# Decode attention with a gated MLP: wq's first block on ScalarE's queue

## The chip, the core and the metric

The kernel runs on one core of a Trainium2 chip. A core has TensorE (matrix multiplications, PE in the profile), VectorE (DVE), ScalarE (ACT), GpSimd (POOL) and SyncE (SP), and 16 DMA engines that move data between the chip's memory and the core's own memory of 128 partitions. SyncE and ScalarE each have a queue on which they issue transfers; in the profile SyncE's is q1 and ScalarE's is q10. The metric is device time in microseconds (us), less is better.

## What is computed

One decode step for 8 sequences: attention over the last 1024 of 4096 cached positions, with 16 query heads on 8 key heads of width 256, and beside it an MLP on the normalised input, mixed by a gate.

```python
# x [8, 1, 448], k_cache and v_cache [8, 8, 4096, 256], wq [448, 4096], wo [4096, 448]
g = _sigmoid((x * gate_w).sum(-1, keepdims=True))
q = (x @ wq).reshape(B, Sq, Hq, Dh).transpose(0, 2, 1, 3)
k = jnp.repeat(k_cache[:, :, Sk - W:, :], rep, axis=1)      # W = 1024, rep = 2
v = jnp.repeat(v_cache[:, :, Sk - W:, :], rep, axis=1)
scores = jnp.einsum("bhqd,bhkd->bhqk", q, k) * (Dh ** -0.5)
o = jnp.einsum("bhqk,bhkd->bhqd", _softmax(scores), v)
a = o.transpose(0, 2, 1, 3).reshape(B, Sq, Hq * Dh) @ wo
y = _layernorm(x)
b = _gelu(y @ w1 + b1) @ w2 + b2
return g * a + (1 - g) * b
```

All tensors are bfloat16.

## The kernel before

Everything large goes through one ring of four slots of 32 KB on each of 128 partitions (4 MB a slot). A list `plan`, filled by `add` (lines 108 to 110), holds the loads in their order: wq; the keys of batch 0; then for each batch b from 1 to 7 its keys and the values of batch b-1; the first MLP weight; the last values and the second MLP weight; wo. `pump` (line 98) issues the loads for which a slot is free, and `done` (line 104), called when the work on a slot has been written, issues the next one; on the chip that load waits until the slot's last reader has finished. So at the start four loads are issued at once: wq, the keys of batches 0 and 1, the values of batch 0. The keys of batch 2 go into wq's slot after the query product, the values of batch 1 into that of batch 0's keys, and so on.

wq has 448 rows. Rows 0 to 383 lie three to a partition (`wq_m`, line 147), so that a partition's three rows are 24 KB in a piece of memory. They are loaded in two pieces (`wq_r`, line 155): the first row of each partition, 8 KB, 1 MB in all; the second and third, 16 KB, 2 MB in all. The last 64 rows, each in two halves, are a third piece (`wq_t`, 4 KB a partition). `rows_loader` (line 137) issues these pieces one behind the other on SyncE's queue; it is also used for the first MLP weight and for wo.

The small inputs are x (8 rows of 896 bytes, line 181) and the gate's row, copied to 8 partitions (line 185), both on ScalarE's queue, and the biases, later, on SyncE's.

`moments` (line 253) brings x into the form that TensorE needs: VectorE copies it into `xs` (lines 228 and 232), transposes it (line 234) and copies the result into `xw` (line 239). It then takes mean and variance, and ScalarE a square root (line 257), for which it loads a table. `query` (line 383) multiplies: 24 matmuls (line 389), the first eight with wq's first piece, the other sixteen with the second, and four (line 401) with the third. ScalarE scales the product (line 411), VectorE transposes it (line 414), both copy it into `qw` (line 427), and `gate` computes the gate from x and the gate's row.

Then, for each batch, TensorE transposes the keys (line 370), ScalarE and VectorE copy the results out of the accumulation memory (lines 376 and 378), GpSimd copies the blocks that VectorE transposed (lines 338 and 346), and TensorE forms the scores (line 435) and, one batch later, the weighted values (line 506). The order of the work on each engine is as written (`manual_schedule`). At the end come the MLP, the product with wo in pieces (lines 662 and 679), the sum (line 689) and the output, half on SyncE's and half on ScalarE's queue (line 691).

Of the kernel before, what the change touches and what calls it, by code (L numbers as in the profile page):

```python
# [17 lines left out]
def kernel(  # L18
# [15 lines left out]
    nc = tc.nc  # L34
# [73 lines left out]
    def add(key, loader):  # L108
        index[key] = len(plan)
        plan.append(loader)  # L110
# [4 lines left out]
    def half_loader(src, b):  # L115
        def load(t):
            for i in range(NG):
                v = src[b, i:Hkv:NG, kv_base:Sk, :].rearrange(
                    "a (s c) d -> s a (c d)", c=NCK
                )  # L120
                nc.sync.dma_start(t[:, i * HS : (i + 1) * HS], v)

        return load
# [10 lines left out]

        return load

    def rows_loader(pieces):
        def load(t):
            o = 0
            for ap in pieces:  # L140
                n = ap.shape[-1]
                nc.sync.dma_start(t[:, o : o + n], ap)  # L142
                o += n

        return load

    wq_m = A_wq[0:DM, :].rearrange("(p r) n -> p (r n)", r=NR)
    wq_t = A_wq[DM:D, :].rearrange("r (h n) -> (r h) n", h=2)
# [6 lines left out]
    wq_r = [wq_m[:, 0:HD], wq_m[:, HD : NR * HD]]  # L155

    def last_values(t):
        pair_loader(A_v_cache, NB - 1, 2)(t)
        nc.sync.dma_start(slot("w12")[:, OW2 : OW2 + FB * D], w2_v)

    add(("wq",), rows_loader(wq_r + [wq_t]))
    add(("k", 0), half_loader(A_k_cache, 0))
    for b in range(1, NB):
        add(("k", b), (half_loader if b == NB - 1 else pair_loader)(A_k_cache, b))
        add(("v", b - 1), pair_loader(A_v_cache, b - 1))
    add(("w12",), rows_loader([w1_m, w1_t]))
    add(("v", NB - 1), last_values)
    cuts = [(q, 0, J8) for q in range(NQW - 2)] + [
# [5 lines left out]
        (NQW - 1, 7, 8),  # L174
    ]
    add(("wo",), rows_loader([wo_v[:, q, j0 * D : j1 * D] for q, j0, j1 in cuts]))

    x_sb = consts.tile([NB, D], BF16)
# [543 lines left out]
```

## Time and profile before

| | |
|---|---|
| time, median of 3 runs | 189.98 us (189.89 to 190.21) |
| profiled execution: its own time | 189.76 us |
| profiled execution: span from the first to the last instruction | 188.0 us |
| busy time TensorE / VectorE / ScalarE / GpSimd | 122.3 / 96.5 / 91.4 / 66.4 us |
| moved by the DMA engines | 77.85 MB, mean 414 GB/s |
| packets on q1 (SyncE) / q10 (ScalarE) | 6712 / 48 |
| TensorE's granted clock, mean share | 0.873 |

The span is what the profile sees on the core; the execution's own time holds what lies around it as well. A busy share is an average over the whole span, so the stages have to be looked at one by one. In a timeline, a row of a "DMA" instruction on ACTq or SPq is the time in which that engine issued the transfer, not the time in which the data moved; an idle time in brackets is followed by what ended it. In the chain of waits, a step "DMA" runs from the issue to the landing and so holds the time in the queue.

### The profile page before, as it was taken

To read this page: it belongs to the slowest core of one execution; us is meant where nothing else is said; L and a number is where in the kernel's file an instruction comes from. 1 tells how busy PE (TensorE), PEld (TensorE's weight loads), DVE (VectorE), ACT (ScalarE), POOL (GpSimd) and SP (SyncE) were. 2 spreads that over 40 slices of the span, in tenths; PEclk is the share of its full clock that TensorE was granted. 3 is DMA by queue.
4 is the path that set the end of the run, shared out by engine and by line. 5 is a ranking of instruction groups with operands and counts; after the bars stand their busy time and mean duration, and the time that the engine had idled before them with its cause. 6 is when DMAs were issued, how large, how long until landed. Compare 5 with 4: busy or idle time off the path is not lost.

```text
span 188.0 us, 2799 instructions
## 1 busy us (share of the span) xinstructions
PE 122.3 (65%) x1104; PEld 79.8 (42%) x1104; DVE 96.5 (51%) x166; ACT 91.4 (49%) x115; POOL 66.4 (35%) x143
## 2 busy tenths in 40 slices
PE   0273099598598447991695948923968885353972
PEld 0022096395296216750684336503853662110221
DVE  7306514754287926740673248713763773763511
ACT  2006879598249255862287059620891994010000
POOL 8000093291069505800398039100991840000000
PEclk9999759969969997999579699995799999955599
DMA  6999999999999999999999999999999999999991
GB/s 211 448 411 439 446 422 422 436 443 422 422 439 424 420 436 439 422 422 439 436 425 425 443 432 418 429 443 436 411 436 446 415 425 428 416 429 441 412 402 54
DMA packets 6771, 77.85 MB, mean 414 GB/s; under 512 B 588, under 2 KB 1128, under 8 KB 1896
## 3 DMA queue, kind: packets, MB, share of 16 engines
q1 hardware_dynamic: 6712, 77.68, 97.3%
q8 instruction: 8, 0.13, 0.2%
q10 hardware_dynamic: 48, 0.02, 0.0%
q14 instruction: 3, 0.02, 0.0%
HBM read 77.69 MB, written 0.01 MB: 413 GB/s over the span
## 4 chain that ended last, share of the span: by engine, by line
DMA 76%; PE 13%; POOL 5%; DVE 2%; ACT 1%; issue 1%; SPq 0%; POOLq 0%; DVEq 0%
DMA slot<-in_A_k_cache_dram 51%; DMA slot<-in_A_v_cache_dram 12%; DMA slot<-in_A_wo_dram 9%; PE ktp L370 8%; POOL kt L346 5%; DMA slot<-in_A_wq_dram 5%; DVE kt L378 1%; PE S_ps L435 1%; ACT kt L376 1%; PE S_ps L389 1%; PE S_ps L401 1%; PE PO L506 1%; DVE B L338 1%; PE S_ps L679 0%; SPq L142 0%
## 5 line engine op out<-in xcount | busy, mean ns | idle before, releaser
L370 PE MATMUL ktp<-ident_f,slot 128*128 128x128 f32 x468 | 73.3, 314 | 33.3 <-DMA slot<-in_A_k_cache_dram 21.2
L346 POOL COPY kt<-B 32x128 f32<-32x128 f32 (+1 forms) x128 | 62.1, 485 | 85.9 <-DVE B L338 80.9
L376 ACT COPY kt<-ktp 128x1024 bf16<-128x1024 bf16 x77 | 73.3, 1030 | 27.4 <-PE ktp L370 27.0
L370 PEld LDWEIGHTS ktp<-ident_f,slot 128*128 128x128 f32 x468 | 61.4, 162 | 47.9 <-issue 21.6
L378 DVE COPY kt<-ktp 128x1024 bf16<-128x1024 bf16 x40 | 27.5, 687 | 19.0 <-PE ktp L370 18.9
L435 PE MATMUL S_ps<-kt,qw 128*4 128x512 bf16 x256 | 17.4, 412 | 7.6 <-POOL kt L346 6.2
L506 PE MATMUL PO<-slot,ET 128*16 128x512 bf16 x256 | 17.5, 416 | 7.3 <-DMA slot<-in_A_v_cache_dram 7.3
L453 ACT ACTIVATE E<-S_ps,nmx 128x1024 f32<-128x1024 f32 x8 | 8.9, 1114 | 22.9 <-DVE nmx L448 22.9
L448 DVE TENSOR_REDUCE nmx<-S_ps 128x1 f32<-128x1024 f32 x8 | 9.8, 1224 | 17.9 <-PE S_ps L435 17.9
L338 DVE STREAM_TRANSPOSE B<-slot 128x512 f32<-128x512 f32 (+1 forms) x8 | 7.3, 908 | 21.2 <-DMA slot<-in_A_k_cache_dram 21.2
L506 PEld LDWEIGHTS <-ET 128*16 128x16 bf16 x256 | 7.1, 94 | 16.8 <-issue 11.0
L435 PEld LDWEIGHTS <-qw 128*4 128x4 bf16 x256 | 5.9, 85 | 16.0 <-issue 10.6
L462 DVE STREAM_TRANSPOSE EB<-E 128x1056 f32<-128x1056 f32 x8 | 10.2, 1278 | 0.3
L389 PE MATMUL S_ps<-slot,xw 128*8 128x512 bf16 x24 | 2.9, 617 | 9.4 <-DVE xw L239 6.0
L522 DVE STREAM_TRANSPOSE T<-PO 128x512 f32<-128x512 f32 x8 | 5.6, 703 | 3.6 <-PE PO L506 3.6
L489 DVE TENSOR_TENSOR ET<-sm,mask 128x512 bf16<-128x512 f32 x8 | 5.5, 692 | 3.4 <-PE sm L481 3.4
L414 DVE STREAM_TRANSPOSE qt<-qs 128x512 bf16<-128x512 bf16 x2 | 1.3, 690 | 8.7 <-ACT qs L411 8.7
L389 PEld LDWEIGHTS <-xw 128*8 128x8 bf16 x24 | 0.6, 100 | 10.7 <-POOL b_r L222 5.9
L584 ACT ACTIVATE zb<-za 128x448 f32<-128x448 f32 x1 | 0.6, 577 | 8.5 <-DVE za L583 8.5
L651 PE MATMUL warm<-slot,ident 128*128 128x512 bf16 (+1 forms) x12 | 4.6, 475 | 0.0
L411 ACT ACTIVATE qs<-S_ps 128x1024 bf16<-128x1024 f32 x1 | 1.0, 1023 | 7.3 <-PE S_ps L401 7.3
L468 DVE SCALAR_TENSOR_TENSOR EZ<-EB,gall 128x128 bf16<-128x128 f32 x8 | 4.0, 495 | 0.0
(81 smaller groups left out, 57.6 us busy)
## 6 DMA issues: line engine op xcount, KB each, us to landing
slot<-in_A_v_cache_dram SPq DMA_DIRECT2D x7, 4096.0 KB, 31.1
slot<-in_A_k_cache_dram SPq DMA_DIRECT2D x6, 4096.0 KB, 37.7
slot<-in_A_k_cache_dram SPq DMA_DIRECT2D x4, 2048.0 KB
slot<-in_A_v_cache_dram SPq DMA_DIRECT2D x2, 2048.0 KB
slot<-in_A_wq_dram SPq DMA_DIRECT2D x1, 2048.0 KB
slot<-in_A_wo_dram SPq DMA_DIRECT2D x2, 896.0 KB
slot<-in_B_w_dram SPq DMA_DIRECT2D x1, 1568.0 KB
slot<-in_B_w_dram SPq DMA_DIRECT2D x1, 1344.0 KB, 22.2
```

The costliest lines, as they stand in the source:

```text
L338: nc.vector.transpose(B[:].rearrange("p c w s a -> p (c w s a)"), kn[:, 0 : n * P],)
L346: nc.gpsimd.tensor_copy(words[BL * w : BL * (w + 1), :, 0:n, g * S8 : (g + 1) * S8, 0], B[BL * g : BL * (g + 1), :, w].rearrange("p c s a ...
L370: nc.tensor.transpose(words[:, c, :, 0], kn[:, o : o + P], ident_f[:])
L376: nc.scalar.copy(dst, src)
L378: nc.vector.tensor_copy(dst, src)
L435: nc.tensor.matmul(S_ps[BL * t : BL * t + UR, n * QN : (n + 1) * QN], lhsT=qw[:, j, b, t, rep * u : rep * u + UR], rhs=KT[u][:, t, n * CQ ...
L448: nc.vector.reduce_max(nmx[:], S_ps[:], axis=AXIS.X, negate=True)
L453: nc.scalar.activation(E[:, 0:W], S_ps[:], ACT.Exp, bias=soft.pop(b)[:], scale=1.0, accum_out=total[:],)
L462: nc.vector.transpose(EB[:].rearrange("p c r -> p (c r)"), E[:])
L489: nc.vector.tensor_tensor(ET[:].rearrange("p c u a r -> p (c u) a r"), sm[:] .rearrange("p k (o r) -> p k o r", o=1) .to_broadcast([P, NCK ...
L506: nc.tensor.matmul(PO[BL * t : BL * t + Hq], lhsT=ET[:, c].rearrange("p u a r -> p (u a r)"), rhs=vn[:, c], start=(c < QD), stop=(c >= NCK ...
L522: nc.vector.transpose(T[:, 0 : NG * n], PO[:].rearrange("p u (e j) -> p u j e", j=J8))
```

## The change

`rows_loader` takes an engine for its first piece, and wq's call names ScalarE. So wq's first piece (128 rows of 8 KB) is issued on ScalarE's queue; since `pump` runs before line 181, it stands ahead of x and the gate's row there. wq's second piece is the first transfer on SyncE's queue. The loads of the first MLP weight and of wo stay wholly on SyncE's queue.

```diff
-    def rows_loader(pieces):
+    def rows_loader(pieces, first=nc.sync):
         def load(t):
             o = 0
-            for ap in pieces:
+            for i, ap in enumerate(pieces):
                 n = ap.shape[-1]
-                nc.sync.dma_start(t[:, o : o + n], ap)
+                eng = nc.sync if i else first
+                eng.dma_start(t[:, o : o + n], ap)
                 o += n
 
         return load
...
-    add(("wq",), rows_loader(wq_r + [wq_t]))
+    add(("wq",), rows_loader(wq_r + [wq_t], nc.scalar))
```

The new lines of `rows_loader` shift the later lines of the file by one.

## The prediction

> **What bounds the kernel now.** I read the page first, then the chain of waits in order of time, then the first 15 us instruction by instruction, because the change touches only transfers issued in the first 2 us.
>
> ```profile
> span 188.0 us, 2799 instructions
> GB/s 211 448 411 439 446 422 422 436 443 422 422 439 424 420 436 439 422 422 439 436 425 425 443 432 418 429 443 436 411 436 446 415 425 428 416 429 441 412 402 54
> q1 hardware_dynamic: 6712, 77.68, 97.3%
> DMA 76%; PE 13%; POOL 5%; DVE 2%; ACT 1%; issue 1%; SPq 0%; POOLq 0%; DVEq 0%
> ```
>
> Each of the 40 slices is 4.7 us. From the second to the last but one the transfers run at 402 to 448 GB/s without a hole, and one queue, q1 (SyncE's), carries 77.68 MB of it at 97.3% of the 16 DMA engines. TensorE, the busiest compute engine, is busy 65% of the span. So the span is: the time until the stream runs, plus 77.7 MB at about 430 GB/s, plus what follows the last byte. The chain shows that tail:
>
> ```profile
> 14.21 37.71 DMA slot<-in_A_k_cache_dram
> ...
> 167.62 16.71 DMA slot<-in_A_wo_dram
> 184.33 0.04 issue
> 184.37 0.88 PE S_ps L679 x12
> ```
>
> The columns are start, duration, what. The last piece of wo lands at 184.33, twelve matmuls end it, and 3.7 us after the landing the span is over. The step at 14.21 is not a 37 us transfer: the keys of batch 2 are issued the moment the query product frees the slot of wq, and queue behind three slots of 4 MB. That queueing is the cover for everything below.
>
> The start, as the timeline has it (start, duration, engine, line, what; in brackets the idle time before it and what ended it):
>
> ```profile
> 0.73 0.59 ACTq L181 DMA_DIRECT2D x_sb<-in_A_x_dram  x1
> 0.73 1.35 SPq L142 DMA_DIRECT2D slot<-in_A_wq_dram  x3
> 2.41 0.54 DVE L228 COPY xs<-x_sb 8x384 bf16<-8x384 bf16 x1
> 5.96 1.02 PE L389 MATMUL S_ps<-slot,xw 128*8 128x512 bf16 x8 [5.96 <-DVE xw L239]
> 10.44 1.88 PE L389 MATMUL S_ps<-slot,xw 128*8 128x512 bf16 x16 [3.46 <-DMA slot<-in_A_wq_dram]
> 12.25 1.92 PE L401 MATMUL S_ps<-slot,xw 128*72 128x512 bf16 x4
> ```
>
> x goes through VectorE from 2.41 to the first matmul at 5.96, 3.55 us. Eight matmuls use wq's first block; the other twenty wait until 10.44 for the second block, so x has slack today. The windows say how the stream comes up (bounds, length, five engines' busy time, clock, DMA share, GB/s):
>
> ```profile
> 1.70:3.00 1.30, 0.00 (x0) 0.00 (x0) 1.25 (x6) 1.25 (x1) 1.30 (x5) 1.00 0.94 212
> 3.00:10.00 7.00, 1.02 (x8) 0.26 (x9) 3.42 (x9) 0.29 (x1) 1.96 (x5) 1.00 0.99 421
> 20.00:50.00 30.00, 23.33 (x205) 17.55 (x205) 13.78 (x24) 22.87 (x29) 12.71 (x32) 0.83 1.00 430
> ```
>
> Nothing moves before 1.70. Against 430 GB/s the ramp loses 1.30 x (1 - 212/430) = 0.66 us, and the 7 us after it 0.15 us: 0.8 us in all is what a perfect start could win.
>
> **The change, part by part.** No byte, no instruction on TensorE, VectorE or GpSimd and no later transfer is added or taken away. Three things move.
>
> *SyncE's queue loses one issue.* Its three wq issues took 1.35 us, so 0.45 each; the second and third and the first four key and value issues come 0.45 us earlier. Worth nothing: behind the first issue there is always a backlog (the last of these transfers ends after 37 us).
>
> *ScalarE's queue gains a 128-row issue at its head.* Estimate 0.4 to 0.6 us, from SyncE's 0.45 and from ScalarE's own first issue of 0.59. x's issue moves from 0.73 to about 1.3, the gate row's from 1.36 to about 1.6, and the table load at 1.67 to about 2. The table is wanted only by the square root at 6.69: hidden. The first byte doesn't move: today both queues issue at 0.73 and their first packets follow in the window 1.70 to 3.00; then too both issue at 0.73. Zero for the stream, with the ramp's own uncertainty from -0.8 (all of its loss is filled) to +0.66 (the second queue pays such a ramp again, on the same engines). I take 0, since nothing in the rows says that the ramp is short of queued work: wq's first block alone gives each engine eight rows of 8 KB, 2.4 us of work.
>
> The Trainium skill (DMA: Bandwidth & Descriptors, section "Issuing engines are not separate DMA queues") says that transfers of all issuing engines end up on the same 16 DMA engines, and that issuing from several saves only sequencer time. By that rule the change saves 0.45 us of issue that nobody waits for, which speaks against a gain; the ramp's 0.8 us is what the rows would still allow.
>
> *x now stands behind 1 MB on its queue, and that megabyte shares the engines with q1.* This is the real cost. What a second queue gets beside q1 is shown by the gate row, issued from 1.36 to 1.64. The packets of ScalarE's queue, q10, from three windows, 1.6 to 1.9, 5.4 to 5.8 and 6.05 to 6.4:
>
> ```profile
> q10 hardware_dynamic: 16, 0.01, 9.0%
> q10 hardware_dynamic: 8, 0.01, 5.1%
> q10 hardware_dynamic: 8, 0.00, 1.3%
> ```
>
> The sixteen early ones are x (eight rows and eight completion writes). The gate's eight rows were served only from 5.4, after wq's first block, and its completions one large packet later. So q10 is not passed over for good, but can wait behind about nine packets of q1, and then gets about every other turn.
>
> An engine moves 430/16 = 26.9 GB/s: 0.305 us for an 8 KB row of wq's first block, 0.61 us for a 16 KB row of its second. Eight rows of each per engine. When x lands:
> - first block served first: 1.7 + 0.66 + 8 x 0.305 = 4.8 us;
> - turn and turn about: 1.7 + 0.66 + 8 x 0.92 = 9.7, and 1.2 for x's row and its completion behind one 16 KB packet each: 10.9 us;
> - q1's eight rows first, as with the gate: 2.4 + 8 x 0.61 + 8 x (0.305 + 0.15 for the 4 KB rows of wq's tail) + 1.2 = 12.1 us.
>
> From x it is 3.55 us to the first matmul and then 28 matmuls without a wait, 1.02 + 1.88 + 1.92 = 4.8 us: the query ends 8.4 us after x, against 14.2 today. First case: no slip. Second: 19.3, a slip of 5.1 us. Third: 20.5, a slip of 6.3. I take the second, and keep 0 and 6.3.
>
> The Trainium skill (the same page, "Queues, rings and completion order") has the engines go round robin between queues at packet granularity. By that, x lands at 10.9; by the gate's row, 12.1; the span is the same by both.
>
> *Where the slip goes.* All of ScalarE's and VectorE's work on q, the transposes of key slots 0 and 1 and so the issues of later slots move by up to 6.3 us. What is late next would be the stream, if a slot were issued after the queue has run dry. The tightest issue, and three rows of how TensorE stands to the stream later:
>
> ```profile
> 45.96 0.65 SPq L131 DMA_DIRECT2D slot<-in_A_k_cache_dram  x1
> 52.05 2.25 PE L370 MATMUL ktp<-ident_f,slot 128*128 128x128 f32 x10 [2.49 <-DMA slot<-in_A_k_cache_dram]
> 71.56 3.78 PE L370 MATMUL ktp<-ident_f,slot 128*128 128x128 f32 x20 [2.16 <-DMA slot<-in_A_k_cache_dram]
> 91.02 5.35 PE L370 MATMUL ktp<-ident_f,slot 128*128 128x128 f32 x24 [5.69 <-DMA slot<-in_A_k_cache_dram]
> ```
>
> When the keys of batch 3 are issued at 45.96, wq's 3.5 MiB and five slots of 4 MiB are queued before them, 24.6 MB; at 430 GB/s from 2.5 us they last until 59.8. Less about 1 us from issue to first packet, 12.8 us remain. A slip of 5.1 uses less than half. TensorE then waits 2.49 us less for batch 2, 2.16 less for batch 3 and the rest, 0.45, is gone at batch 4. From 91 us on nothing differs. Cost 0; without this cover it would be 5.1 us.
>
> Sum: span 188.0 + 0, with the 1.76 around it 189.76, the profiled execution's own time. The median shown, 189.98, is 0.22 above that: forecast 190.0.
>
> **The rivals.**
> - *The ramp fills.* Two queues put twice the reads in flight while the first packets come back, and 0.4 to 0.8 us of the loss goes: 189.2 to 189.6, middle 189.4. For it: 212 GB/s in that stretch. Against: x's sixteen packets were in that ramp too, and q1 had work queued on every engine. Chance 0.17.
> - *A second ramp* (slower). The second queue pays its start on the same engines, in the place of q1's packets: +0.4 to +0.66 us, 190.4 to 190.6. For it: the 1.70 to 3.00 row has no cause that the trace shows. Against: the gate's rows at 5.4 left the rate of 3 to 10 at 421. Chance 0.15.
> - *The stream runs dry* (slower). If q10 gets one packet in four, not in two, its eight rows take 8 x (0.305 + 3 x 0.61) = 17.1 us, x lands at 2.4 + 17.1 + 3.7 = 23.2 and the slip is 17.4. It decides from a slip of 12.8, that is from x landing at 18.6; past that every microsecond shows: 17.4 - 12.8 = +4.6, 194.6. For it: the gate waited behind nine packets. Against: its completion waited behind one. Chance 0.10.
>
> **How the numbers follow.** Forecast "hidden", 190.0, chance 0.58. A measurement of this kernel can tell about 0.2% (0.38 us) from no change; only the ramp rival is faster by more (0.17), the second ramp and the dry stream are slower (0.25). The range goes from 190.0 - 0.8 = 189.2 to 190.0 + 0.66 + 0.2 for the spread of the runs shown = 190.9, and leaves the dry stream outside.
>
> **What would show it.** Right: in the changed profile x's copy on VectorE starts near 11 us and not at 2.41, the query ends near 19, the keys of batch 2 are issued there, the GB/s row has no hole, and TensorE's wait for batch 2 is shorter or gone while the wait for batch 4 is as before. The ramp rivals are read from the GB/s of 1.70 to 10. Wrong: a slice under 400 GB/s near 60 us, or a different landing of wo's last piece.

## The result, and the profile after

The changed kernel takes 190.31 us (median of 15 runs), the kernel before in the same series 189.97 us (15 runs): a ratio of 1.0018, with a 95% interval of 1.0011 to 1.0025. That is 0.34 us slower: less than the 0.2% that the prediction took as the least that can be told from no change, but over these 15 runs the interval leaves out 1. The profiled execution took 190.5 us, its span 188.8.

From the page of the changed kernel, lines as in the prediction:

```profile
span 188.8 us, 2798 instructions
GB/s 198 432 421 441 424 437 424 441 427 424 434 430 429 422 431 430 434 434 424 427 441 424 434 427 434 431 420 437 434 431 427 424 437 421 416 427 437 418 385 29
q1 hardware_dynamic: 6568, 76.63, 95.7%
q10 hardware_dynamic: 192, 1.07, 1.4%
DMA 56%; PE 22%; DVE 8%; POOL 5%; ACT 4%; issue 2%; ACTq 0%; DVEq 0%; POOLq 0%
```

The stream still has no hole, and q10 now carries wq's first block. The first slice is lower (198 for 211). The share of DMA in the chain of waits fell from 76% to 56%, since the chain now goes through x, the query and TensorE's work up to 62 us, where it had the 37.71 us step of the keys of batch 2 before. Such a step holds the time in the queue, so the fall doesn't mean that less time is bound by the stream: the GB/s row is as full as it was.

Six rows of the changed kernel's start, from its timeline:

```profile
1.17 0.59 ACTq L182 DMA_DIRECT2D x_sb<-in_A_x_dram  x1
11.21 0.61 SPq L131 DMA_DIRECT2D slot<-in_A_v_cache_dram  x1
11.49 0.54 DVE L229 COPY xs<-x_sb 8x384 bf16<-8x384 bf16 x1 [8.97 <-DMA x_sb<-in_A_x_dram]
14.06 2.73 PE L390 MATMUL S_ps<-slot,xw 128*8 128x512 bf16 x24 [14.06 <-DVE xw L240]
16.73 1.92 PE L402 MATMUL S_ps<-slot,xw 128*72 128x512 bf16 x4
18.68 0.61 SPq L131 DMA_DIRECT2D slot<-in_A_k_cache_dram  x1
```

x, issued at 1.17, reaches VectorE at 11.49, not at 2.41. The 28 matmuls then run without a wait, the query ends at 18.65, and the keys of batch 2 are issued at 18.68, not at 14.21: a slip of 4.5 us. The same slip two batches on, and where it ends:

```profile
50.37 0.65 SPq L131 DMA_DIRECT2D slot<-in_A_k_cache_dram  x1
...
53.91 2.93 PE L371 MATMUL ktp<-ident_f,slot 128*128 128x128 f32 x20
...
71.84 1.50 PE L371 MATMUL ktp<-ident_f,slot 128*128 128x128 f32 x12 [0.75 <-DMA slot<-in_A_k_cache_dram]
91.80 3.43 PE L371 MATMUL ktp<-ident_f,slot 128*128 128x128 f32 x15 [6.97 <-DMA slot<-in_A_k_cache_dram]
```

The keys of batch 3 are issued at 50.37 (before 45.96), still 4.4 us late. TensorE's wait for batch 2 is gone (2.49 before), that for batch 3 is 0.75 (2.16), and at batch 4 TensorE waits again, longer than before (6.97 for 5.69): it is ahead of the stream, and the stream itself is late. So the slip is not seen in the loss; e2 below tests that. Two windows of the changed kernel, with the bounds used before:

```profile
3.00:10.00 7.00, 0.00 (x0) 0.00 (x0) 0.00 (x0) 0.41 (x1) 1.87 (x5) 1.00 0.97 408
20.00:50.00 30.00, 19.01 (x142) 16.26 (x141) 15.79 (x38) 23.93 (x35) 12.83 (x32) 0.77 1.00 430
```

From 3 to 10 us the engines moved 408 GB/s, not 421: 7 x 13/430 = 0.2 us lost. (The windows and the GB/s row count a row of a transfer where it starts.) From 20 us on the rate is the same 430. The end of the chain of waits:

```profile
168.27 16.77 DMA slot<-in_A_wo_dram
185.05 0.04 issue
185.09 0.89 PE S_ps L680 x12
```

wo's last piece lands at 185.05, before at 184.33; the tail behind it is unchanged. This execution is 0.19 us above its kernel's median, so its 0.72 is more than the typical loss.

What the packets' own records in the trace say is used in the experiments. The first row that each engine moved took 520 to 1085 ns in the kernel before (8 KB; 309 ns later on), and 856 to 1767 ns in the changed one (16 KB, from q1; 611 ns later on), with rows of q10 up to 1024 ns behind it. And the completions of the second half of batch 0's keys, one for each engine, spread from 20.69 to 21.03 us before and from 20.70 to 21.70 after. The first engine is no later; the last one is 0.67 us later, near the 0.72 by which wo's last piece is later. When the keys of batch 1 land near 31 us, the spread between the first and the last engine is still the same, 0.34 us before and 1.00 after: an engine that falls behind in the ramp stays behind.

### The profile page after: what moved, and what is told of

It reads as the page before. It is cut to its first block, busy times and chain, and to the rows that moved or that the text cites. A ratio compares the mean times of both kernels' runs of the same rounds, so it can differ in the third digit from the quotient of the medians.

```text
span 188.8 us, 2798 instructions
## 1 busy us (share of the span) xinstructions
PE 120.4 (64%) x1104; PEld 78.1 (41%) x1104; DVE 94.6 (50%) x166; ACT 90.8 (48%) x115; POOL 66.7 (35%) x143
## 4 chain that ended last, share of the span: by engine, by line
DMA 56%; PE 22%; DVE 8%; POOL 5%; ACT 4%; issue 2%; ACTq 0%; DVEq 0%; POOLq 0%
DMA slot<-in_A_k_cache_dram 30%; PE ktp L371 14%; DMA slot<-in_A_v_cache_dram 12%; DMA slot<-in_A_wo_dram 9%; DMA x_sb<-in_A_x_dram 5%; POOL kt L347 5%; DVE kt L379 4%; PE S_ps L436 3%; PE PO L507 2%; PE S_ps L390 1%; ACT qw L428 1%; ACT kt L377 1%; PE S_ps L402 1%; DVE B L339 1%; DVE qt L415 1%
## 5 line engine op out<-in xcount | busy, mean ns | idle before, releaser
L371 PE MATMUL ktp<-ident_f,slot 128*128 128x128 f32 x468 | 70.3, 305 | 32.0 <-DMA slot<-in_A_k_cache_dram 16.1
L371 PEld LDWEIGHTS ktp<-ident_f,slot 128*128 128x128 f32 x468 | 58.9, 157 | 45.7 <-issue 18.2
L507 PE MATMUL PO<-slot,ET 128*16 128x512 bf16 x256 | 18.3, 430 | 7.1 <-DMA slot<-in_A_v_cache_dram 7.1
L436 PE MATMUL S_ps<-kt,qw 128*4 128x512 bf16 x256 | 18.1, 429 | 6.9 <-POOL kt L347 6.9
L229 DVE COPY xs<-x_sb 8x384 bf16<-8x384 bf16 x1 | 0.5, 541 | 9.0 <-DMA x_sb<-in_A_x_dram 9.0
```

What stands on the lines that cost most here:

```text
L371: nc.tensor.transpose(words[:, c, :, 0], kn[:, o : o + P], ident_f[:])
L436: nc.tensor.matmul(S_ps[BL * t : BL * t + UR, n * QN : (n + 1) * QN], lhsT=qw[:, j, b, t, rep * u : rep * u + UR], rhs=KT[u][:, t, n * CQ ...
L507: nc.tensor.matmul(PO[BL * t : BL * t + Hq], lhsT=ET[:, c].rearrange("p u a r -> p (u a r)"), rhs=vn[:, c], start=(c < QD), stop=(c >= NCK ...
```

## The experiments

Each ratio is against the kernel before in the same series, with its 95% interval.

### One part at a time

**e1**, x and the gate's row ahead of wq's first block on ScalarE's queue:

```diff
     x_sb = consts.tile([NB, D], BF16)
-    pump()
     nc.scalar.dma_start(x_sb[:], xf)
...
     nc.scalar.dma_start(g_b[:], ...)
+    pump()
```

> x and the gate's row stand ahead of wq's first block on ScalarE's queue; wq is still on two queues. The changed kernel measured 1.0018 of the one before, and in its profile 7 us from 3.0 on ran at 408 GB/s, not 421. Theory A (the large piece at the head of SyncE's queue: the first packet of an engine is 16 KB, not 8 KB, and takes 0.9 to 1.8 us, not 0.5 to 1.1): SyncE's queue still begins with 16 KB rows, so 1.001 to 1.002. Theory B (two bulk queues in the ramp cost a second start): 1.001 to 1.002. Theory C (x late, and with it the slip of 4.5 us of the work up to batch 4): x lands near 2 us, so 1.000. By all three the first matmul is at about 6 us and the query ends between 14 and 16 us.

Measured: 1.0009 (1.0001 to 1.0018). Half of the loss, though x is early; the query ends at 16.1 us, not within the 14 to 16 expected.

**e2**, one bulk queue, x late:

```diff
-    add(("wq",), rows_loader(wq_r + [wq_t]))
+    def wq_then_x(t):
+        rows_loader(wq_r + [wq_t])(t)
+        nc.sync.dma_start(x_sb[:], xf)
+        nc.sync.dma_start(g_b[:], ...)
+    add(("wq",), wq_then_x)
...
-    nc.scalar.dma_start(x_sb[:], xf)
...
-    nc.scalar.dma_start(g_b[:], ...)
```

> All of wq on SyncE's queue in the old order, x and the gate's row behind it on the same queue; ScalarE's queue is empty until the output. x lands near 11 us and the query ends near 19 us, as in the changed kernel, but one queue does the ramp and its first packets are 8 KB. Theory A: 1.000. Theory B: 1.000. Theory C: 1.0018, the whole of the changed kernel's loss.

Measured: 1.0001 (0.9992 to 1.0010). In its timeline x and the query are as late as in the changed kernel:

```profile
11.97 0.54 DVE L231 COPY xs<-x_sb 8x384 bf16<-8x384 bf16 x1 [9.45 <-DMA x_sb<-in_A_x_dram]
...
19.16 0.60 SPq L131 DMA_DIRECT2D slot<-in_A_k_cache_dram  x1
```

A slip of 4.95 us, a little more than the change's own, costs nothing that can be measured. Theory C falls.

**e3**, one queue, wq's second block ahead of its first:

```diff
-    add(("wq",), rows_loader(wq_r + [wq_t]))
+    def wq_second_first(t):
+        nc.sync.dma_start(t[:, HD : NR * HD], wq_r[1])
+        nc.sync.dma_start(t[:, 0:HD], wq_r[0])
+        nc.sync.dma_start(t[:, NR * HD : NR * HD + HD // 2], wq_t)
+    add(("wq",), wq_second_first)
```

> All of wq on SyncE's queue, its 16 KB rows ahead of its 8 KB rows; x as before on ScalarE's queue, landing near 2 us. Theory A: 1.001 to 1.002 though there is one bulk queue and no slip. Theory B: 1.000. Theory C: 1.000. The eight matmuls that use the first block now wait for it with the others until about 10 us, so the query may end 1 us later than 14.2, which costs nothing by any of the three.

Measured: 1.0009 (1.0000 to 1.0018): a loss without a second queue and without a late x, if a small one; its interval reaches down to no loss.

**e4**, two queues, the 8 KB rows on SyncE's, the 16 KB rows on ScalarE's behind x and the gate's row:

```diff
-    add(("wq",), rows_loader(wq_r + [wq_t]))
+    def wq_two_queues(t):
+        nc.sync.dma_start(t[:, 0:HD], wq_r[0])
+        nc.scalar.dma_start(t[:, HD : NR * HD], wq_r[1])
+        nc.sync.dma_start(t[:, NR * HD : NR * HD + HD // 2], wq_t)
+    add(("wq",), wq_two_queues)
...
-    pump()
     nc.scalar.dma_start(x_sb[:], xf)
...
     nc.scalar.dma_start(g_b[:], ...)
+    pump()
```

> wq's 8 KB rows first on SyncE's queue, its 16 KB rows on ScalarE's queue behind x and the gate's row: two bulk queues, x early, and the first packet of an engine is 8 KB. Theory A: 1.000. Theory B: 1.001 to 1.002. Theory C: 1.000.

Measured: 1.0001 (0.9992 to 1.0009). The second bulk queue does no harm, although the wait for the 16 KB rows delays the query to 20.0 us. It was issued 0.9 us after the first (two small issues stand ahead of it), but its rows came far later: the first 16 KB row of q10 starts at 5.45 us, and in e1 the first 8 KB row of q10 at 5.62, when q1's first started near 1.8. What q10 had from 2 to 5.4 us in e1, in e4 and in the changed kernel:

```profile
q10 hardware_dynamic: 6, 0.00, 0.3%
q10 hardware_dynamic: 13, 0.01, 0.6%
q10 hardware_dynamic: 43, 0.35, 27.7%
```

So e1 and e4 don't have two bulk queues in the ramp at all. By these four, theory A, the row size at the head, seemed to hold. But e1 and e3 gave half of the loss only, and neither e1 nor e4 tested a second queue in the ramp.

### Both heads at once

**e8** is the changed kernel again.

> The changed kernel itself, in the same series as the next three. The series before left three shares: large rows at the head alone 1.0009 (e1, e3), x late alone 1.0001 (e2), two bulk queues with a small head and a second queue that starts 0.9 us later 1.0001 (e4). All theories: 1.0018 as before, 1.0011 to 1.0025, and a stream that runs 0.25 to 0.30 us later than the one before from 4 us on.

Measured: 1.0020 (1.0011 to 1.0029). The ratio came as expected, the stream not quite: it moved 278 GB/s from 1.7 to 4 us, the kernel before 298, and both 422 from 4 to 10, so it ran 2.3 x 20/430 = 0.1 us late, not 0.25 to 0.30.

**e5**, e4 with wq's second block ahead of x on ScalarE's queue:

```diff
-    add(("wq",), rows_loader(wq_r + [wq_t]))
+    def wq_two_heads(t):
+        nc.sync.dma_start(t[:, 0:HD], wq_r[0])
+        nc.scalar.dma_start(t[:, HD : NR * HD], wq_r[1])
+        nc.sync.dma_start(t[:, NR * HD : NR * HD + HD // 2], wq_t)
+    add(("wq",), wq_two_heads)
```

> wq's 8 KB rows at the head of SyncE's queue and its 16 KB rows at the head of ScalarE's, ahead of x: both bulk queues start at once, x lands near 11 us, and the queue that is served first begins with 8 KB rows. Theory A (row size at the head of the queue that is served first): 1.000. Theory B, as it now stands (two bulk queues that start at once, in the same ramp): 1.0015 to 1.0025.

Measured: 1.0023 (1.0014 to 1.0032). From e4 it differs in a late x, which alone was free, and in when q10's rows come: the first 16 KB row starts at 2.31 us, not at 5.45. Theory A, as row size of the queue served first, falls; B holds.

**e6**, the changed kernel with 4 KB rows at the head of SyncE's queue:

```diff
-    wq_r = [wq_m[:, 0:HD], wq_m[:, HD : NR * HD]]
+    wq_r = [
+        wq_m[:, 0:HD],
+        wq_m[:, HD : HD + HD // 2],
+        wq_m[:, HD + HD // 2 : NR * HD],
+    ]
```

> The changed kernel with wq's second block cut in two: 4 KB rows at the head of SyncE's queue, then 12 KB rows. Both bulk queues still start at once. Theory A: the loss goes, 1.000 to 1.0005. Theory B: 1.0015 to 1.0025.

Measured: 1.0023 (1.0013 to 1.0033). Smaller rows at one head do not give the loss back. The query ends at 15.6 us here, so a slip of 1.4 goes with the full loss: once more the slip is not it.

**e7**, the kernel before with 2 KB rows at the head:

```diff
-    wq_r = [wq_m[:, 0:HD], wq_m[:, HD : NR * HD]]
+    wq_r = [
+        wq_m[:, 0 : HD // 4],
+        wq_m[:, HD // 4 : HD],
+        wq_m[:, HD : NR * HD],
+    ]
```

> The kernel before with wq's first block cut in two on SyncE's queue: 2 KB rows at the head, then 6 KB rows; x as before. Theory A, if smaller heads go on paying: the ramp loses 0.1 to 0.3 us less, 0.9985 to 0.9995. Theory B: 1.000, since there is one bulk queue as before.

Measured: 1.0019 (1.0010 to 1.0028). A miss for both theories: one queue, and slower. A part is plain: a 2 KB row took 84 ns and a 6 KB row 234, against 77 and 232 at the rate of the 8 KB rows (309 ns); eight of each per engine make 0.07 us. The rest was not measured by itself; the first 2 KB rows took up to 480 ns, and the rows of the second piece, too, began slowly, with up to 724 ns for 6 KB between 2.6 and 3.4 us.

### The cover, the late x again, and the size of the head

**e9** makes x later still, to find where a slip begins to cost:

```diff
-    add(("k", 0), half_loader(A_k_cache, 0))
+    def k0_then_x(t):
+        half_loader(A_k_cache, 0)(t)
+        nc.sync.dma_start(x_sb[:], xf)
+        nc.sync.dma_start(g_b[:], ...)
+    add(("k", 0), k0_then_x)
...
-    nc.scalar.dma_start(x_sb[:], xf)
...
-    nc.scalar.dma_start(g_b[:], ...)
```

> Tests the cover of 12.8 us. One bulk queue as in the kernel before; x and the gate's row stand on SyncE's queue behind wq and the keys of batch 0, so that x lands at about 20.7 us and everything behind the query slips by about 14.9 us. The prediction's account: a slip over 12.8 us lets the stream run dry once, where the keys of batch 3 are issued (near 61 us, first packet near 62, the queue empty near 60): +2.0 us, 1.008 to 1.013, and a hole in the GB/s row near 60 us. Rival: the cover is larger than I worked out, 1.000 to 1.002 without a hole. Rival: a slip costs its own length, 1.07 or more.

Measured: 1.0124 (1.0091 to 1.0158), 192.35 us for 189.87. A row of its timeline, and the GB/s row of its page (span 191.1):

```profile
59.12 0.66 SPq L131 DMA_DIRECT2D slot<-in_A_k_cache_dram  x1
```

```profile
GB/s 219 440 424 429 432 429 432 439 439 425 415 436 314 412 430 429 432 425 429 425 439 432 425 432 432 429 425 429 436 432 432 429 432 410 424 431 428 419 317 8
```

The keys of batch 3 are issued 13.2 us late, and the thirteenth slice, 57.3 to 62.1 us, has the one hole, 314: 4.8 x 116/430 = 1.3 us, and 0.2 in the next slice. That is the dry stream, close to where the account of the cover put it. By 12.8 us of cover a slip of 13.2 would leave the engines without rows for 0.4 us; it was about 0.9, as a mean over the sixteen. Most engines ran out near 59.7 us, and the first row of the new keys starts at 60.57, 1.45 us after its issue and not about 1, so the cover was nearer 12.3. The rest of the hole is a slow start: the first rows took 851 to 962 ns on most engines, against 611 later on. Of the 2.5 us that the kernel lost, the hole explains 1.5; the rest was not followed up.

**e10**, the changed kernel with x and the gate's row on GpSimd's queue:

```diff
-    nc.scalar.dma_start(x_sb[:], xf)
+    nc.gpsimd.dma_start(x_sb[:], xf)
...
-    nc.scalar.dma_start(
+    nc.gpsimd.dma_start(
         g_b[:], gate_w.rearrange("(o d) -> o d", o=1).to_broadcast([NB, D])
```

> The changed kernel with x and the gate's row issued on GpSimd's queue: both bulk queues still start at once, but x lands before 6 us and nothing slips. Theory B (two bulk queues that start at once): 1.0015 to 1.0025, as with the changed kernel. If the late x has a share in the loss that shows only together with two queues: 1.0005 to 1.001.

Measured: 1.0042 (1.0030 to 1.0055), more than either expected. VectorE had x at 8.19 us, not before 6, so this run doesn't take the slip away, it shortens it. Its span, 188.7 us, is about that of the changed kernel, 188.8; its profiled execution took 190.46, as the changed one's 190.5. The issues on GpSimd also delay the set-up of its tiles (`ident` from 0.73 to 2.42 us), which the change does not. What the median of 190.69 has beyond that was not explained, and the run settles little.

**e11**, one queue, one piece of 24 KB rows at the head:

```diff
-    wq_r = [wq_m[:, 0:HD], wq_m[:, HD : NR * HD]]
+    wq_r = [wq_m]
```

> All of wq on SyncE's queue, its rows 0 to 383 as one piece of 24 KB a partition; x as before. One bulk queue, one piece in the ramp. Theory A (row size at the head): 1.0009 or more. Theory E (what counts is how many pieces are opened while the ramp lasts, to about 4 us: one in the kernel before, two in the changed kernel and in e5, e6 and e7): 1.000 to 1.0005.

Measured: 1.0026 (1.0016 to 1.0037). One queue and one piece, and the largest loss with x early: theory E falls. The first rows took 916 to 2249 ns. The window from 3 to 10 us of e11:

```profile
3.00:10.00 7.00, 0.00 (x0) 0.08 (x1) 3.42 (x10) 0.29 (x1) 1.96 (x5) 1.00 0.94 401
```

and that of e2, which lost nothing:

```profile
3.00:10.00 7.00, 0.00 (x0) 0.00 (x0) 0.00 (x0) 0.00 (x0) 1.87 (x5) 1.00 1.00 422
```

401 GB/s with one large head, 422 with a small one and x late. Much of this difference is the counting: the 24 KB rows that were under way at 3.00 are not in e11's 401. From 1.7 to 10 us the two moved nearly the same, 312 x 2.3 + 414 x 6 = 3202 KB in e11 and 289 x 2.3 + 425 x 6 = 3215 KB in e2. The loss shows in the slowest engine, below. With the ratio, e11 says that neither the second queue nor the late x is needed for the loss.

**e12**, the changed kernel with every row of the two blocks 8 KB:

```diff
-    wq_r = [wq_m[:, 0:HD], wq_m[:, HD : NR * HD]]
+    wq_r = [wq_m[:, r * HD : (r + 1) * HD] for r in range(NR)]
```

> The changed kernel with wq's second block cut into its two rows of 8 KB: both bulk queues still start at once, but every row at either head has 8 KB, as in the kernel before. Theory B (two heads at once, whatever the rows): 1.0015 to 1.0025. Theory F (what counts is how many bytes of large rows each engine is given at once in the ramp: 8 KB in the kernel before and 1.000, 16 KB in e3 and 1.0009, 24 KB in the changed kernel, e5 and e11 and 1.002 to 1.0026): here 16 KB, so 1.0005 to 1.0012. Theory A (row size alone): 1.000.

Measured: 1.0013 (1.0004 to 1.0022). Just beside the range of F and inside the interval of both B and F: inconclusive between these two; A, with 1.000, is outside.

### All together

The second column and the fourth come from the packets' records of one execution each: how large a row each engine is given at once at the head of its queues, and when the slowest engine had its part of the second half of batch 0's keys. The last column is that execution's own time.

| run | KB at the heads | ratio | slowest engine, us | own time, us |
|---|---|---|---|---|
| before | 8 | 1 | 21.03 | 189.76 |
| e4 (second queue's rows from 5.45 us) | 8 | 1.0001 | 21.16 | 189.96 |
| e2 (x late) | 8 | 1.0001 | 21.25 | 189.96 |
| e1 (second queue's rows from 5.62 us) | 16 | 1.0009 | 21.20 | 189.88 |
| e3 | 16 | 1.0009 | 21.31 | 190.05 |
| e12 | 8 + 8 | 1.0013 | 21.34 | 190.14 |
| e8, changed kernel | 8 + 16 | 1.0020 | 21.47 | 190.17 |
| changed kernel | 8 + 16 | 1.0018 | 21.70 | 190.50 |
| e5 | 8 + 16 | 1.0023 | 21.84 | 190.55 |
| e10 | 8 + 16 | 1.0042 | 21.49 | 190.46 |
| e11 | 24 | 1.0026 | 21.68 | 190.51 |
| e6 | 8 + 4 | 1.0023 | 21.62 | 190.45 |
| e7 | 2 | 1.0019 | 21.69 | 190.28 |

e9 is left out, since its loss is the hole near 60 us. In twelve of the thirteen rows the own time less the time in the fourth column is 168.6 to 168.8 us. So all losses but a part of e10's (169.0) are there at 21 us, and what happens later adds next to nothing. It is the slowest engine that counts: less the mean over the sixteen engines, the same twelve own times lie between 168.9 and 169.5. With rows of 8 KB and more, the loss grows with the bytes that an engine has under way at once in the ramp: 8, 16, 24 KB. The two runs with smaller rows, e6 and e7, don't fit that, and why the first rows are slow at all was not found. Whether two heads at once cost more than one head of the same bytes was not settled either: e12, with 16 KB in two heads, and e3, with 16 KB in one, overlap in their intervals.

## Why the prediction was right, and which step was off

- *The stream bounds the kernel.* Right: 430 GB/s from 20 to 50 us in both, no hole, the tail as it was.
- *When x lands.* "10.9" by turn and turn about; VectorE had it at 11.49. The trace shows the turns: between 3.5 and 9.5 us q1 moved 106 large rows and q10 102, one for one. This agrees with the Trainium skill (DMA: Bandwidth & Descriptors, "Queues, rings and completion order"), which has the engines go round robin between queues. The other case, taken from the gate's row, where q1's eight rows go first, did not occur here, where both queues were issued at 0.73. A wait of that kind did occur in e1 and e4: issued 0.9 us later, the second queue's large rows started only at 5.62 and 5.45 us. So in these runs it went by the moment of issue which of the two cases held, a condition that the prediction did not have; why it does is not shown.
- *The slip.* 5.1 forecast, 4.5 measured, because the first of the 28 matmuls came 2.57 us after the copy of x began, not 3.55: the two copies of line 232 took 1.26 us before and 0.28 now. That x was 0.6 us later than forecast hides a part of this miss.
- *The cover.* Right in kind, and tested from both sides: 4.95 us of slip free in e2, a hole in e9 when the keys of batch 3 came 13.2 us late. Its length, 12.8 us as worked out, was about 12.3, since 1.45 us and not 1 passed from the issue to the first row. The slip was gone at batch 3, one batch sooner than forecast.
- *SyncE's issues 0.45 us earlier.* Right for three of four (1.65 for 2.13, 2.94 for 3.43). The values of batch 0 were issued at 11.21, not at 4.11, since SyncE then waited for a transfer of wq to complete. The queue held enough; it cost nothing. On ScalarE's queue the gate row's issue moved from 1.36 to 1.79, not to "about 1.6": the prediction's own 0.4 to 0.6 us gives 1.8 to 2.0.
- *"Zero for the stream."* This is the term that was mis-sized: it measured +0.34 us. Both ends had been kept (-0.8 and +0.66), and 0 was taken since the ramp had enough queued. It had; the mistake was to ask what more queued work could win in the ramp and not what a larger head costs there. The rival of the second ramp had the place and the sign, at 0.4 to 0.66; but its cause, a second queue, is not needed, as e11 shows. The median of 190.31 lies nearer that rival's 190.4 to 190.6, which had a chance of 0.15, than the forecast of 190.0; the range holds it because its upper end was drawn for this rival.
- *The signs.* x's copy near 11, the query's end near 19, the missing hole and the shorter wait for batch 2 came as named. Two did not: wo's last piece landed 0.72 us later, which the prediction had named as a sign of being wrong, and TensorE's wait for batch 4 grew from 5.69 to 6.97 us. The first is the stream's loss in the ramp; in the second that loss meets a TensorE that was ready 0.5 us earlier (at 84.8, not at 85.3).

The Trainium skill's rule that issuing from several engines saves only issue time (the same page, "Issuing engines are not separate DMA queues") spoke rightly against a gain: no run gained. It says nothing of a loss, and there is one.

No run was faster than the kernel before; e4 and e2 equal it.

## What to carry to other kernels

Where a stream bounds the kernel and its queue is deep, late work behind it is free until the slip exceeds the queue: work out that length in us and compare, as here 4.5 with about 12. But what this stream lost in its first microseconds it did not make up, and it was the slowest DMA engine that counted. So keep the first transfer's rows at the size that measured best (8 KB here, of 2, 8, 16 and 24 KB on one queue), and try other bulk transfers on a second queue a microsecond later: issued 0.9 us later, as in e4, they cost nothing here, but their rows also came only at 5.45 us.

## What was not expected

Cutting the head of the stream finer did not make it faster: 2 KB rows on one queue were slower than the kernel before (1.0019), and 4 KB rows on one of two queues no better than the changed kernel (1.0023 for 1.0018 and 1.0020). And the changed kernel doesn't leave the same spread between the engines each time: 1.00 us in its first profiled execution, 0.68 in e8, and e4, which lost nothing, has 0.61. So the spread alone doesn't tell the loss; the time at which the slowest engine has its part does.
